# Alternating the first x tiles and the wq/wk slices over two DMA queues, with staggered query steps and gate_w turned on TensorE

## The chip, the cores and the metric

The kernel runs on one core of one Trainium2 chip. The metric is the device time of a run in microseconds (us); lower is better. In the first job the runs of one kernel agree within some tenths of a per cent; in others before alone spread over 1%, and jobs (on different chips of the same kind) can differ too, so times are compared only within one job. TensorE is called PE, VectorE DVE, ScalarE ACT, GpSimd POOL and SyncE SP, as the profile has them.

## The reference, cut to what matters

```python
# x: [1, 2048, 640], wqkv: [640, 1920], gate_w: [640], all bf16
g = sigmoid((x * gate_w).sum(-1))
q, k, v = split(x @ wqkv)            # 32 heads of 20
pq, pk = phi(q), phi(k)              # phi(t) = (t+1 if t>0 else exp(t)) + 1e-6
a = ((pq @ (pk^T v)) / (pq @ sum(pk))) @ wo
b = x1 + gelu(layernorm(x1) @ w3) @ w4,  x1 = x + shifted_gelu_mlp(x)
out = g * a + (1 - g) * b
```

The change touches only how `x @ wq` and `x @ wk` start, and how the column `gate_w` gets beside `wk`, so that the key matmul also gives `x @ gate_w`.

## The kernel before

x is worked on in 16 tiles of 128 tokens. A tile is turned (transposed in five blocks of 128) on PE, evacuated to `xT` by DVE, and then multiplied with five slices of `wq`, 128 rows each; one product of one tile with one slice is a "step" (t, k) of two matmuls, 512 and 128 columns wide, 0.27 us at full rate. The first four tiles are handled slice by slice as the loads land (`q_four`); later tiles come through DMA transposes.

```python
    sch.dma("act", junk[...], A_wqkv[...], "touch")        # 2.5 KB read, result unused
    dma_in(x_tok[:, 0, :], x2[0:128, :], "x0")             # dma_in: on SyncE's queue
    dma_in(x_tok[:, 1, :], x2[128:256, :], "x1")
    load_wq(0)
    dma_in(x_tok[:, 2:4, :], x2[256:512, :]..., "x23")     # x tiles 2 and 3 in one load
    for k in range(1, KD): load_wq(k)
    for k in range(KD): dma_in(wkg[:, k, 0:D], A_wqkv[128 * k:..., D:2 * D], "wk%d" % k)
    dma_in(wkg[:, :, D + 2:D + 3], gate_w..., "gw", noncontig=True)      # 640 pieces of 2 bytes
    # ... cut: the other x tiles, 4 at a time, and their DMA transposes

    WARM = 3200                       # columns of warm-up matmuls on a tile of ones
    def t_x(t):                       # turn x tile t on PE, evacuate it by one DVE copy
        b = bank()
        tr_group(b, [x_tok[:, t, 128 * k:128 * (k + 1)] for k in range(KD)])
        copy(dve, xT[:, :, 128 * t:128 * (t + 1)], psb(b, 0, D)...)

    def q_four():   # (t, k): step of tile t with slice k; (t, None): t_x(t); (None, None): filler matmuls
        order = [(0, 0), (None, None), (1, 0), (2, None), (3, None), (0, 1), (1, 1), (2, 0), (0, 2), (1, 2), (3, 0),
                 (0, 3), (1, 3), (0, 4), (2, 1), (1, 4), (2, 2), (2, 3), (2, 4), (3, 1), (3, 2), (3, 3), (3, 4)]
    # ... cut: warm-up, t_x(0), t_x(1), filler, q_four(), then the key steps of tile 0, and the rest of the kernel
```

## Time and profile before

| what | value | view |
|---|---|---|
| median of 3 runs | 262.18 us (261.81 to 262.46) | times |
| span of the profiled run | 260.0 us | page |
| PE busy | 254.7 us, 98% | page, part 1 |
| PE in the chain that ended last | 97% | page, part 4 |
| first key step begins | 11.26 us | timeline |

From the page: the span, and busy time, share and instruction count of each engine.

```profile
span 260.0 us, 4263 instructions
## 1 busy us (share of the span) xinstructions
PE 254.7 (98%) x1671; PEld 135.9 (52%) x1703; DVE 148.9 (57%) x266; ACT 106.9 (41%) x215; POOL 96.8 (37%) x151
```

The head in the timeline of PE before: start, duration in us, engine, line, what is written from what, number of instructions; in brackets the idle time before and what ended it. L830 are the warm-up and filler matmuls, L611 the turning of x tiles, L857/L858 the two matmuls of a step.

```profile
1.05 2.85 PE L830 MATMUL ps<-xn 128*128 128x512 bf16 x7 [1.05 <-POOL xn L659]
3.69 1.21 PE L611 MATMUL ps<-ident,x_tok 128*128 128x128 bf16 x10
4.73 0.27 PE L830 MATMUL ps<-xn 128*128 128x128 bf16 x2
5.11 0.38 PE L857 MATMUL ps<-wq,xT 128*128 128x512 bf16 x1
...
5.77 0.72 PE L611 MATMUL ps<-ident,x_tok 128*128 128x128 bf16 x10
6.32 0.38 PE L857 MATMUL ps<-wq,xT 128*128 128x512 bf16 x1
...
11.26 0.38 PE L857 MATMUL ps<-wkg,xT 128*128 128x512 bf16 x1
```

Durations overlap, since matmuls are pipelined; the distance from one start to the next is what a thing costs. Ten turned blocks take 1.04 us from 3.69, and 0.55 us from 5.77: PE goes over to twice the rate in between. From 6.32 on, steps follow each other every 0.27 us. After this head the waits view of PE lists only 0.5 us of waiting up to the end, so only what happens before the first key step, and at the tail, can move the end.

The loads of the first 8 us in the DMA view of before: what, queue, count, KB of one, median us from issue to landing.

```profile
wq<-in_A_wqkv_dram SPq DMA_DIRECT2D x5, 160.0 KB, 3.8
...
x_tok<-in_A_x_dram SPq DMA_DIRECT2D x2, 160.0 KB, 2.5
x_tok<-in_A_x_dram SPq DMA_DIRECT2D x1, 320.0 KB, 3.5
```

Taken one by one (issue plus time to landing, good to about 0.1 us), x0 lands at 3.4 us, x1 at 3.6, wq0 at 4.8, x2 and x3 together at 5.7, wq1 at 6.1, wq4 at 7.9.

### The profile page before, as it was taken

To read this page: it belongs to the slowest core of one execution; us is meant where nothing else is said; L and a number is where in the kernel's file an instruction comes from. 1 tells how busy PE (TensorE), PEld (TensorE's weight loads), DVE (VectorE), ACT (ScalarE), POOL (GpSimd) and SP (SyncE) were. 2 spreads that over 40 slices of the span, in tenths; PEclk is the share of its full clock that TensorE was granted. 3 is DMA by queue.
4 is the path that set the end of the run, shared out by engine and by line. 5 is a ranking of instruction groups with operands and counts; after the bars stand their busy time and mean duration, and the time that the engine had idled before them with its cause. 6 is when DMAs were issued, how large, how long until landed. Compare 5 with 4: busy or idle time off the path is not lost.

```text
span 260.0 us, 4263 instructions
## 1 busy us (share of the span) xinstructions
PE 254.7 (98%) x1671; PEld 135.9 (52%) x1703; DVE 148.9 (57%) x266; ACT 106.9 (41%) x215; POOL 96.8 (37%) x151
## 2 busy tenths in 40 slices
PE   8999999999999999999999999999999999999996
PEld 4555555555555454555444545554455544455553
DVE  1597877899903799979994407992033410143333
ACT  1496777741355757674874240005500045100000
POOL 5013995859874017865854202230011100021001
PEclk9999999999999999999999999999999999999999
DMA  6855989642566894355565700232000020000311
GB/s 199 255 103 143 211 149 158 194 87 23 105 126 103 275 377 94 76 101 58 107 124 109 125 0 0 45 85 74 3 0 0 3 101 0 3 0 0 103 50 50
DMA packets 50691, 24.82 MB, mean 95 GB/s; under 512 B 42052, under 2 KB 49261, under 8 KB 50672
## 3 DMA queue, kind: packets, MB, share of 16 engines
q1 hardware_dynamic: 49280, 21.15, 35.8%
q0 software_dynamic: 1152, 3.28, 5.2%
q8 instruction: 13, 0.21, 0.3%
q10 hardware_dynamic: 240, 0.13, 0.2%
q14 instruction: 6, 0.05, 0.1%
HBM read 12.05 MB, written 2.62 MB: 56 GB/s over the span
## 4 chain that ended last, share of the span: by engine, by line
PE 97%; issue 1%; DVE 1%; POOL 0%; POOLq 0%
PE ps L600 61%; PE ps L1106 21%; PE ps L781 8%; PE ps L857 2%; PE ps L830 1%; PE ps L1020 1%; PE ps L1088 1%; DVE x_tok L639 1%; PE ps L858 1%; PE ps L611 1%; PE ps L934 1%; PE ps L1085 0%; POOL xn L659 0%; POOLq L1249 0%
## 5 line engine op out<-in xcount | busy, mean ns | idle before, releaser
L600 PE MATMUL ps<-xnT,w 128*128 128x512 bf16 x349 | 80.7, 379 | 0.5
L1106 PE MATMUL ps<-w,h2T 128*128 128x128 bf16 (+1 forms) x409 | 57.9, 298 | 0.7 <-issue 0.5
L656 ACT ACTIVATE h2T<-ps 128x512 bf16<-128x512 f32 x52 | 30.5, 600 | 65.6 <-PE ps L600 65.5
L600 PEld LDWEIGHTS ps<-xnT,w 128*128 128x128 bf16 x360 | 33.9, 98 | 36.9 <-issue 0.4
L639 DVE SCALAR_TENSOR_TENSOR x_tok<-ps,stg,abx 128x512 bf16<-128x512 f32 (+1 forms) x32 | 17.2, 551 | 61.6 <-PE ps L1106 61.6
L622 POOL TENSOR_SCALAR abx<-x_tok,stg 128x640 f32<-128x640 bf16 x16 | 14.8, 923 | 100.6 <-DVE x_tok L639 95.1
L1106 PEld LDWEIGHTS ps<-w,h2T 128*128 128x128 bf16 x416 | 32.4, 98 | 25.6 <-issue 1.1
L622 POOL TENSOR_SCALAR xn<-x_tok,st 128x640 bf16<-128x640 bf16 x32 | 36.8, 1155 | 15.4 <-DMA xnT<-xn 14.9
L656 ACT ACTIVATE Er<-ps 128x640 bf16<-128x640 f32 x32 | 22.4, 704 | 17.4 <-PE ps L600 8.5
L655 ACT ACTIVATE junk<-x_tok 128x640 bf16<-128x640 bf16 x32 | 23.6, 737 | 4.9 <-DVE x_tok L637 4.4
L656 ACT ACTIVATE hsT<-ps 128x512 bf16<-128x512 f32 (+1 forms) x32 | 18.9, 593 | 15.1 <-PE ps L600 12.7
L600 PE MATMUL ps<-w,hsT 128*128 128x512 bf16 (+1 forms) x159 | 23.8, 298 | 0.1
L600 PE MATMUL ps<-M_sb,pqnT 128*128 128x128 bf16 (+1 forms) x156 | 23.5, 297 | 0.3
L781 PE MATMUL ps<-pk_tok,x_tok 128*128 128x128 bf16 (+1 forms) x156 | 23.3, 297 | 0.2
L639 DVE SCALAR_TENSOR_TENSOR abx<-ps,stg,abx 128x640 f32<-128x640 f32 x16 | 14.1, 884 | 15.3 <-PE ps L600 15.3
L600 PE MATMUL ps<-wkg,xT 128*128 128x512 bf16 (+1 forms) x147 | 22.3, 298 | 0.2
L600 PEld LDWEIGHTS ps<-w,hsT 128*128 128x128 bf16 x160 | 13.3, 98 | 12.3
L600 PEld LDWEIGHTS ps<-M_sb,pqnT 128*128 128x128 bf16 x160 | 13.1, 98 | 10.4
L600 PE MATMUL ps<-wq,xT 128*128 128x512 bf16 (+1 forms) x119 | 18.2, 298 | 0.1
L622 DVE TENSOR_SCALAR Er<-Er 128x640 bf16<-128x640 bf16 x32 | 12.0, 376 | 9.1 <-ACT Er L656 8.8
L637 DVE SCALAR_TENSOR_TENSOR x_tok<-ps,x_tok 128x640 bf16<-128x640 f32 x16 | 13.1, 821 | 6.9 <-PE ps L600 6.0
L600 PEld LDWEIGHTS ps<-wkg,xT 128*128 128x128 bf16 x150 | 12.2, 97 | 9.0
(71 smaller groups left out, 230.0 us busy)
## 6 DMA issues: line engine op xcount, KB each, us to landing
w<-in_B_w_dram SPq DMA_DIRECT2D x1, 2160.0 KB, 8.2
w<-in_B_w_dram SPq DMA_DIRECT2D x1, 2080.0 KB, 13.7
x_tok<-in_A_x_dram SPq DMA_DIRECT2D x3, 640.0 KB, 5.7
out_dram<-x_tok SPq DMA_DIRECT2D x3, 640.0 KB, 3.5
w<-in_B_w_dram POOLq DMA_DIRECT2D x8, 160.0 KB, 4.8
wq<-in_A_wqkv_dram SPq DMA_DIRECT2D x5, 160.0 KB, 3.8
wkg<-in_A_wqkv_dram SPq DMA_DIRECT2D x5, 160.0 KB, 3.9
wv<-in_A_wqkv_dram POOLq DMA_DIRECT2D x1, 800.0 KB, 6.2
```

The source lines that it names most:

```text
L600: ins = e.matmul(out_ap, l, r, start=(i == 0), stop=(i == n - 1))
L611: ins = e.transpose(o, s_, ident[:])
L622: return engf(lambda e: e.tensor_scalar(out_ap, in_ap, s1, s2, op0, op1), rd, [out_ap], cost=cost)
L637: return dve(lambda e: e.scalar_tensor_tensor(out_ap, in0, scalar, in1, op0, op1, accum_out=accum), rd, [out_ap, accum], cost=cost + 70.0)
L639: return dve(lambda e: e.scalar_tensor_tensor(out_ap, in0, scalar, in1, op0, op1), rd, [out_ap], cost=cost)
L655: return act(lambda e: e.activation(out_ap, in_ap, func, bias=bias, scale=scale, accum_out=accum), rd, wr, cost=cost)
L656: return act(lambda e: e.activation(out_ap, in_ap, func, bias=bias, scale=scale), rd, wr, cost=cost)
L781: ins = e.matmul(o, l, r, start=(t0 + q_ == 0), stop=(t0 + q_ == NT - 1))
L830: ins = e.matmul(ps[:, b, 0:n], xn[:, 0, 0:128], xn[:, 0, 0:128].unsqueeze(1).to_broadcast([128, n // 128, 128]), start=True, stop=True)
L857: e.matmul(ps[:, b, 0:512], l, w[:, k, 0:512], start=(k == 0), stop=(k == KD - 1))
L858: return e.matmul(ps[:, b + 1, 0:n2], l, w[:, k, 512:512 + n2], start=(k == 0), stop=(k == KD - 1))
L1106: ins = e.matmul(o, l, r, start=False, stop=(i == KFF - 1), skip_group_check=(n0 > 0))
```

## The change

Intent: fill both issuing queues and let tiles and slices land in the order in which PE wants them, so that PE has steps to do earlier; save the strided gate_w load and the touching read; start the warm-up at once.

```diff
-    sch.dma("act", junk[...], A_wqkv[...], "touch")
-    dma_in(x_tok[:, 0, :], ..., "x0");  dma_in(x_tok[:, 1, :], ..., "x1");  load_wq(0)
-    dma_in(x_tok[:, 2:4, :], ..., "x23")
-    for k in range(1, KD): load_wq(k)
-    for k in range(KD): dma_in(wkg[:, k, 0:D], ..., "wk%d" % k)
-    dma_in(wkg[:, :, D + 2:D + 3], gate_w..., "gw", noncontig=True)
+    sch.dma("pool", gwr[0:KD, :], gate_w.rearrange("(k p) -> k p", p=128), "gw")
+    for t in range(4):
+        load_x(t)                                   # SyncE
+        load_w(wq, "wq", t, 0, "act")               # ScalarE
+    load_w(wq, "wq", 4, 0, "sp")
+    for k in range(KD):
+        load_w(wkg, "wk", k, D, "sp" if k % 2 else "act")
+    for t in range(4, 8): load_x(t)                 # single tiles, then their transposes
...
-    WARM = 3200
+    WARM = 2944
     def t_x(t):
-        # five blocks, one DVE copy
+        for ks in ((0,), (1, 2, 3, 4)) if t < 2 else (range(KD),):
+            # turn the blocks ks into a bank; for t == 3 also gwr as a 5-column matmul into the same bank
+            copy(dve, xT[:, ks[0]:ks[-1] + 1, ...], ...)
+            # for t == 3: copy(dve, wkg[:, :, D + 2:D + 3], ...)
...
     # warm-up and filler: operands are now a ready constant tile of ones, not a tile that POOL writes first
-    order = [(0, 0), (None, None), (1, 0), (2, None), (3, None), (0, 1), (1, 1), (2, 0), (0, 2), ...]
+    order = [(0, 0), (0, 1), (1, 0), (1, 1), (2, None), (0, 2), (2, 0), (1, 2), (2, 1), (3, None), (0, 3), (1, 3), (3, 0), ...]
-    # t_x(0), t_x(1), filler
+    # t_x(0), filler, t_x(1)
```

A comparison of the two programs' instruction order shows that PE does the same things in the same order after these steps.

More of the change, by code (lines that the diff above doesn't have):

```diff
@@ L464, in psb @@
         return ps[:, b, :].bitcast(BF16)[:, n0:n1]
-    ones_c = pa.alloc("ones_c", [128, 768], BF16)
+    ones_c = pa.alloc("ones_c", [128, 128], BF16)
     ident = pa.alloc("ident", [128, 128], BF16)
@@ L470, in _build @@
     negh = pa.alloc("negh", [128, 4], F32)
+    gwr = pa.alloc("gwr", [8, 128], BF16)
     st1 = pa.alloc("st1", [128, 8, NT], F32)
@@ L674, in dma_in, with load_x, load_w, x_transpose @@
         return sch.dma("sp", out_ap, in_ap, key, **kw)
-    sch.dma("act", junk[0:16, 0, 0:80].rearrange("p (k f) -> p k f", k=KD),
-            A_wqkv[:, 0:16].rearrange("(k e r) f -> e r k f", k=KD, r=8)[:, 0, :, :], "touch")
-    dma_in(x_tok[:, 0, :], x2[0:128, :], "x0")
-    dma_in(x_tok[:, 1, :], x2[128:256, :], "x1")
-    def load_wq(k):
-        dma_in(wq[:, k, :], A_wqkv[128 * k:128 * (k + 1), 0:D], "wq%d" % k)
-    load_wq(0)
-    dma_in(x_tok[:, 2:4, :], x2[256:512, :].rearrange("(n p) d -> p n d", p=128), "x23")
-    for k in range(1, KD):
-        load_wq(k)
-    for k in range(KD):
-        dma_in(wkg[:, k, 0:D], A_wqkv[128 * k:128 * (k + 1), D:2 * D], "wk%d" % k)
-    dma_in(wkg[:, :, D + 2:D + 3], gate_w.rearrange("(k p o) -> p k o", p=128, o=1), "gw", noncontig=True)
-    for c in range(1, NCH):
+    def load_x(t):
+        dma_in(x_tok[:, t, :], x2[128 * t:128 * (t + 1), :], "x%d" % t)
+    def load_w(dst, name, k, c0, queue):
+        sch.dma(queue, dst[:, k, 0:D], A_wqkv[128 * k:128 * (k + 1), c0:c0 + D], "%s%d" % (name, k))
+    def x_transpose(t):
+        sch.dma("sp", xT[:, :, 128 * t:128 * (t + 1)], x_tok[:, t, :], "trx%d" % (t % 4), transpose=True)
+    sch.dma("pool", gwr[0:KD, :], gate_w.rearrange("(k p) -> k p", p=128), "gw")
[3 more added lines that the diff above has]
+    load_w(wq, "wq", 4, 0, "sp")
+    for k in range(KD):
+        load_w(wkg, "wk", k, D, "sp" if k % 2 else "act")
+    for t in range(4, 8):
+        load_x(t)
+    for t in range(4, 8):
+        x_transpose(t)
+    for c in range(2, NCH):
         dma_in(x_tok[:, 4 * c:4 * c + 4, :], x2[512 * c:512 * (c + 1), :].rearrange("(n p) d -> p n d", p=128), "xc%d" % c)
         for t in range(4 * c, 4 * c + 4):
-            sch.dma("sp", xT[:, :, 128 * t:128 * (t + 1)], x_tok[:, t, :], "trx%d" % (t % 4), transpose=True)
+            x_transpose(t)
     k_done = {}
@@ L716, in load_wvo @@
             sch.dma("pool", wo_aug[0:n, r, :], A_wo[R6 * r:R6 * r + n, :], "wo", group_total=6, deps=dp)
-    memset(pool, xn[:, 0, 0:128], 1.0)
     memset(pool, ones_c[:], 1.0)
@@ L740, in _build @@
     IT = _Items()
-    WARM = 3200
+    WARM = 2944
     WARM2 = 256
     def t_x(t):
-        b = bank()
-        tr_group(b, [x_tok[:, t, 128 * k:128 * (k + 1)] for k in range(KD)])
-        src = psb(b, 0, D).rearrange("p (k c) -> p k c", k=KD)
-        dst = xT[:, :, 128 * t:128 * (t + 1)]
-        copy(dve, dst, src)
+        for ks in ((0,), (1, 2, 3, 4)) if t < 2 else (range(KD),):
+            b = bank()
+            tr_group(b, [x_tok[:, t, 128 * k:128 * (k + 1)] for k in ks])
+            if t == 3:
+                pe(lambda e: e.matmul(ps[:, b, 448:448 + KD], gwr[0:KD, :], ident[0:KD, 0:KD], start=True, stop=True),
+                   [gwr[0:KD, :], ident[:]], [ps[:, b, 448:448 + KD]], cost=60.0)
+            copy(dve, xT[:, ks[0]:ks[-1] + 1, 128 * t:128 * (t + 1)],
+                 psb(b, 0, 128 * len(ks)).rearrange("p (k c) -> p k c", k=len(ks)))
+            if t == 3:
+                copy(dve, wkg[:, :, D + 2:D + 3], ps[:, b, 448:448 + KD].rearrange("p (k o) -> p k o", o=1))
     def phi(b, dst, after_exp=None):
@@ L829, in fn @@
             for n in steps:
-                ins = e.matmul(ps[:, b, 0:n], xn[:, 0, 0:128], xn[:, 0, 0:128].unsqueeze(1).to_broadcast([128, n // 128, 128]), start=True, stop=True)
+                ins = e.matmul(ps[:, b, 0:n], nc.const_aps.tensor(1.0, [128, 128], BF16), nc.const_aps.tensor(1.0, [128, n], BF16),
+                               start=True, stop=True)
             return ins
-        pe(fn, [xn[:, 0, 0:128]], [ps[:, b, :]], cost=cols * cyc)
+        pe(fn, [], [ps[:, b, :]], cost=cols * cyc)
     def q_tile(t):
@@ L864, in q_four @@
     def q_four():
-        order = [(0, 0), (None, None), (1, 0), (2, None), (3, None), (0, 1), (1, 1), (2, 0), (0, 2), (1, 2), (3, 0), (0, 3), (1, 3), (0, 4),
-                 (2, 1), (1, 4), (2, 2), (2, 3), (2, 4), (3, 1), (3, 2), (3, 3), (3, 4)]
+        order = [(0, 0), (0, 1), (1, 0), (1, 1), (2, None), (0, 2), (2, 0), (1, 2), (2, 1), (3, None), (0, 3), (1, 3), (3, 0), (0, 4),
+                 (2, 2), (1, 4), (2, 3), (2, 4), (3, 1), (3, 2), (3, 3), (3, 4)]
         stream(order, wq, 128, lambda t, b: phi(b, pq_tok[:, t + 1, :]))
@@ L879, in _build @@
     addA(("warm",), 0.0, lambda: warmup(WARM, 0.834))
-    for i in range(2):
-        addA(("tx", i), 0.28, lambda i=i: t_x(i))
+    addA(("tx", 0), 0.28, lambda: t_x(0))
     addA(("warm", 1), 0.0, lambda: warmup(WARM2, 0.42))
+    addA(("tx", 1), 0.28, lambda: t_x(1))
     addA(("q", 3), 5.44, q_four)
```

## The prediction

> **What bounds the kernel.** TensorE. The page's busy table has PE at 254.7 us of a 260.0 us span (98%), the clock row shows full grant, and PE has 97% of the chain that ended last. The waits view gives PE 1.1 us for POOL at the start and 0.5 us of issue. Only time saved at head or tail moves the end. The change touches the head; a comparison of instruction order shows PE's order unchanged after the query steps of the first four tiles.
>
> **The head today (timeline).** PE fills with warm-up matmuls from 1.05 to 3.7 us while x tiles 0 and 1 land (issued 0.79 and 1.23 us, 2.4 to 2.6 us to landing). Ten transposes run from 3.69 to 4.73, about 104 ns each; the next ten, from 5.77, take 0.56 us, so PE was at half rate in the first group. The Trainium skill ("TensorE: Matmul & The Clock Gate", What's actually happening) has the array at half clock until about 3.4 us of sustained work; the trace agrees, the change falling between 3.69 and 5.1 us. Then come two fillers, a gap before 5.11, a step, a filler, a step; PE is dense only from 5.77. The first key step starts at 11.23 after 0.19 us idle: it also waits for gate_w, issued at 6.97 with 4.2 us to landing, so about 11.17.
>
> **Removed, added, moved.** Useful PE work from the first transpose to the first key step: 20 transposes and 20 steps of 0.27 us, about 7.0 us; today it takes 7.5. Removable: 0.5 us of fillers, gaps and gate wait, plus 0.2 to 0.3 us because the warm-up reads a ready constant and begins near 0.8 us, so full clock comes earlier too. Against it: one filler stays (0.1 to 0.2 us), a 5-column matmul (under 0.05 us), three small DVE copies.
> Loads: SyncE issued 11 small loads, 0.43 us each, up to 6.97 us. With two queues the last wq slice is issued near 2.6 instead of 4.1 us. But transfers share one bandwidth (345 GB/s from 4 to 8 us, DMA view; 0.47 us per 164 KB slice), and the Trainium skill ("DMA: Bandwidth & Descriptors", Issuing engines are not separate DMA queues) says a second issuer saves only issue time. So x0 lands at 3.3 to 3.5 us as now, x1 later (near 4.1, sharing with wq0), wq4 near 7.0: just ahead of the staggered steps.
> gate_w through GpSimd costs about 0.9 us of POOL (eight w1 loads took 7.20), so the identity is ready near 2.3 us, not 2.0: harmless. ScalarE issues seven loads to about 4 us; its first exp is due near 8.5. Tiles 4 to 7 are transposed earlier than 13.16 us; PE did not wait for them.
>
> **On the critical path:** the first key step at about 10.6 us instead of 11.23, everything behind it 0.6 us earlier.
>
> **Prediction:** 261.6 us, 261.0 to 262.3 in 8 of 10 cases. Faster by over 2%: 0.01; within 2%: 0.98; slower by over 2%: 0.01.
>
> **What will show it.** Warm-up from about 0.8 us; first transposes at 3.3 to 3.5; first query step near 4.7; first key step at 10.3 to 10.9 without a gate_w wait; last PE instruction earlier by as much. DMA view: first loads issued before 5 us, rate still near 345 GB/s.
>
> **What would make it wrong.** x1 or wq1 landing after 4.5 us, through sharing with wq0, or because the small touching read of wqkv was of use (3.05 to 4 us has only about 140 GB/s); a gap that lowers the PE clock; the identity later than 3.4 us; DVE evacuation holding the staggered steps.

## The result, and the profile after

The changed kernel took 262.81 us (median of 6 runs, 262.46 to 263.89), before took 262.25 us (6 runs, 261.81 to 262.7). The ratio is 1.0026 with a 95% interval of 1.0006 to 1.0047: slower by a quarter of a per cent, where 0.2% faster had been forecast. (Ratios here are the mean time of one kernel's fast runs over that of the other's of the same rounds, so not quite the ratio of the quoted medians.)

The page after:

```profile
span 261.1 us, 4300 instructions
## 1 busy us (share of the span) xinstructions
PE 257.3 (99%) x1703; PEld 135.7 (52%) x1703; DVE 149.2 (57%) x269; ACT 106.8 (41%) x215; POOL 96.0 (37%) x151
```

PE's busy time rose by 2.6 us, but that is no finding: 32 more PE records are in this trace, and some matmul records can be missing from a trace. The timeline of PE after tells more (L841 is warm-up and filler, L612 the turning of x tiles, L869/L870 a step, L755 the gate_w matmul):

```profile
0.83 2.61 PE L841 MATMUL ps<-const-bfloat16-1.0 128*128 128x512 bf16 x8 [0.83 <-PEq L1261]
3.81 0.71 PE L612 MATMUL ps<-ident,x_tok 128*128 128x128 bf16 x5 [0.36 <-DMA x_tok<-in_A_x_dram]
...
4.53 0.69 PE L612 MATMUL ps<-ident,x_tok 128*128 128x128 bf16 x5
5.06 0.38 PE L869 MATMUL ps<-wq,xT 128*128 128x512 bf16 x1
...
6.40 0.45 PE L612 MATMUL ps<-ident,x_tok 128*128 128x128 bf16 x5
6.69 0.38 PE L869 MATMUL ps<-wq,xT 128*128 128x512 bf16 x1
...
7.44 0.39 PE L869 MATMUL ps<-wq,xT 128*128 128x512 bf16 x1 [0.32 <-DVE xT L666]
...
8.27 0.44 PE L612 MATMUL ps<-ident,x_tok 128*128 128x128 bf16 x5
8.64 0.17 PE L755 MATMUL ps<-ident,gwr 5*128 5x5 bf16 x1
8.75 0.39 PE L869 MATMUL ps<-wq,xT 128*128 128x512 bf16 x1
...
9.49 0.39 PE L869 MATMUL ps<-wq,xT 128*128 128x512 bf16 x1
...
12.31 0.38 PE L869 MATMUL ps<-wkg,xT 128*128 128x512 bf16 x1
```

The first key step begins at 12.31 us instead of 11.26, 1.05 us later. The last group of PE begins at 255.32 instead of 254.26 us, 1.06 us later. So the whole loss of this profile arose before the first key step, and nothing was won or lost behind it. The last group, before and then after:

```profile
254.26 3.69 PE L1106 MATMUL ps<-w,h2T 128*128 128x512 bf16 x26
```

```profile
255.32 3.69 PE L1118 MATMUL ps<-w,h2T 128*128 128x512 bf16 x26
```

One caution: a profile is one draw. The profiled run of before took 261.42 us, less than any of its six runs in the first job; e10 below, with the same loads and steps, has its first key step at 12.00 us. So 1.05 us is what separates these two profiles, not the loss of a typical run (0.56 us between the medians).

Where it arose can be read from starts. The first query step begins at 5.06 us (5.11 before): equal. From there to the first key step, 20 steps and two groups of turned blocks need 20 x 0.27 + 2 x 0.29 = 6.0 us at full rate. Before took 6.15 us for it, after 7.25. The excess of 1.2 us after is made up of these gaps, each a start less the preceding start and cost:

| gap | us | what ended it |
|---|---|---|
| before x tile 2 is turned (6.14 to 6.40) | 0.26 | x2 lands at 6.3 to 6.4 |
| before step (2,0) (6.96 to 7.44) | 0.48 | the DVE copy of x tile 2, begun at 6.89, 0.49 us long |
| from the end of x tile 3's turning to step (0,3) (8.55 to 8.75) | 0.20 | the gate_w matmul |
| before step (3,0) (9.30 to 9.49) | 0.19 | the DVE cast of gate_w, right behind the DVE copy of x tile 3 |
| before the first key step (12.22 to 12.31) | 0.09 | issue |

The DVE copies of x tiles 2 and 3, the cast, and the weight load of PE that opens step (3,0):

```profile
6.89 0.49 DVE L666 COPY xT<-ps 128x640 bf16<-128x640 bf16 x1 [1.21 <-PE ps L612]
8.85 0.49 DVE L666 COPY xT<-ps 128x640 bf16<-128x640 bf16 x1 [1.47 <-PE ps L755]
9.26 0.17 DVE L666 CAST wkg<-ps 128x5 bf16<-128x5 f32 x1
9.49 0.10 PEld L869 LDWEIGHTS ps<-wq,xT 128*128 128x128 bf16 x1 [0.36 <-DVE wkg L666]
```

Queues in the DMA view, 6 to 8 us, before and then after (packets, MB, share of the time of the 16 engines):

```profile
DMA packets 599, 0.68 MB, mean 340 GB/s; under 512 B 68, under 2 KB 599, under 8 KB 599
...
q1 hardware_dynamic: 599, 0.68, 103.7%
```

```profile
DMA packets 627, 0.71 MB, mean 355 GB/s; under 512 B 73, under 2 KB 627, under 8 KB 627
...
q1 hardware_dynamic: 312, 0.35, 51.6%
q10 hardware_dynamic: 315, 0.36, 50.8%
```

One queue already had the engines busy all the time; two queues share the same bandwidth in equal halves. That agrees with the Trainium skill ("DMA: Bandwidth & Descriptors", Queues, rings and completion order), by which each DMA engine goes round-robin over the queues that have work, packet by packet, and the rate is close to the limit of about 358 GB/s that the same page gives for one core's memory reads (Specifications): 355 is measured here, though 362 in e8 below, so the figure is no hard bound. So x0 shares with wq0 and lands at 3.8 us instead of 3.4, x1 at 4.5 instead of 3.6, x2 at 6.3 and x3 at 7.3 instead of 5.7; wq1 lands at 4.7 instead of 6.1, and wq4 at 8.1 instead of 7.9.

### The profile page after: what moved, and what is told of

Same layout as the page of the kernel before. It is cut to its first block, busy times and chain, and to the rows that moved or that the text cites. A ratio compares the mean times of both kernels' runs of the same rounds, so it can differ in the third digit from the quotient of the medians.

```text
span 261.1 us, 4300 instructions
## 1 busy us (share of the span) xinstructions
PE 257.3 (99%) x1703; PEld 135.7 (52%) x1703; DVE 149.2 (57%) x269; ACT 106.8 (41%) x215; POOL 96.0 (37%) x151
## 4 chain that ended last, share of the span: by engine, by line
PE 96%; DMA 2%; DVE 1%; SPq 0%; issue 0%
PE ps L601 61%; PE ps L1118 21%; PE ps L792 8%; PE ps L869 2%; DMA x_tok<-in_A_x_dram 2%; PE ps L1032 1%; PE ps L1100 1%; DVE x_tok L640 1%; PE ps L946 1%; PE ps L870 0%; SPq L285 0%; PE ps L612 0%; DVE xT L666 0%; PE ps L1097 0%; PE ps L755 0%
## 5 line engine op out<-in xcount | busy, mean ns | idle before, releaser
L601 PE MATMUL ps<-xnT,w 128*128 128x512 bf16 x360 | 82.3, 379 | 0.0
L1118 PE MATMUL ps<-w,h2T 128*128 128x512 bf16 (+1 forms) x416 | 58.8, 299 | 0.0
L623 POOL TENSOR_SCALAR xn<-x_tok,st 128x640 bf16<-128x640 bf16 x32 | 35.6, 1120 | 15.4 <-DMA xnT<-xn 14.9
L601 PE MATMUL ps<-M_sb,pqnT 128*128 128x512 bf16 (+1 forms) x160 | 24.3, 299 | 0.0
L792 PE MATMUL ps<-pk_tok,x_tok 128*128 128x512 bf16 (+1 forms) x160 | 23.9, 299 | 0.0
L792 PEld LDWEIGHTS ps<-pk_tok,x_tok 128*128 128x128 bf16 x160 | 12.4, 98 | 8.4
```

Of the source, the lines that this page charges most:

```text
L601: ins = e.matmul(out_ap, l, r, start=(i == 0), stop=(i == n - 1))
L623: return engf(lambda e: e.tensor_scalar(out_ap, in_ap, s1, s2, op0, op1), rd, [out_ap], cost=cost)
L792: ins = e.matmul(o, l, r, start=(t0 + q_ == 0), stop=(t0 + q_ == NT - 1))
L1118: ins = e.matmul(o, l, r, start=False, stop=(i == KFF - 1), skip_group_check=(n0 > 0))
```

## The experiments

Eighteen runs, of fourteen new kernels and of the changed one again, were made in five jobs (e3b repeats e3, e4b repeats e4, e16 repeats e13). All results were correct against the reference. "Key" is the start of the first key step in the profiled run, "full" the time from which PE's matmuls are seen at full rate (a 512-column matmul listed at 0.38 us and followed after 0.22, not at 0.63 and after 0.43).

| job | kernel | median us (range; runs) | ratio to before (95%) | key | full |
|---|---|---|---|---|---|
| 1 | before | 262.25 (261.81-262.7; 6) | | 11.26 | 4.7 |
| 1 | changed | 262.81 (262.46-263.89; 6) | 1.0026 (1.0006-1.0047) | 12.31 | 5.0 |
| 2 | before | 262.96 (261.7-267.17; 7) | | | |
| 2 | e1_oldorder | 264.96 (263.4-265.84; 4) | 1.0062 (0.9984-1.014) | 13.15 | 4.5 |
| 2 | e2_onequeue | 263.98 (262.96-264.61; 4) | 1.0027 (0.996-1.0095) | 14.36 | 9.9 |
| 2 | e3_split | 262.3 (261.94-263.3; 4) | 0.9979 (0.9899-1.0058) | 11.69 | 4.3 |
| 2 | e4_oldloads | 262.95 (262.03-453.89; 4) | 0.998 (0.9901-1.006) | (clock 0.56) | |
| 3 | before | 262.34 (262.06-266.19; 11) | | | |
| 3 | e4b_oldloads | 262.28 (262.06-263.05; 6) | 0.9977 (0.9937-1.0017) | 12.02 | by 5.3 |
| 3 | e5_gwold | 262.49 (262.11-263.86; 4) | 0.9989 (0.9926-1.0053) | 12.87 | 7.1 |
| 3 | e6_bridge | 262.82 (262.66-263.05; 4) | 0.9995 (0.9946-1.0044) | 12.43 | 5.3 |
| 3 | e7_notouch | 262.28 (262.02-262.6; 6) | 0.9975 (0.9935-1.0014) | 12.17 | by 5.4 |
| 4 | before | 263.08 (262.25-266.22; 11) | | | |
| 4 | e8_again | 264.0 (263.06-264.92; 6) | 1.0039 (1.0011-1.0066) | 13.94 | 8.5 |
| 4 | e3b_split | 264.01 (262.31-264.38; 6) | 1.0036 (1.0008-1.0064) | 11.95 | 5.9 |
| 4 | e9_split_gwold | 263.1 (262.38-263.99; 6) | 1.0005 (0.9979-1.0031) | 12.65 | 7.4 |
| 4 | e10_warmup | 263.28 (261.77-263.7; 6) | 1.0005 (0.9976-1.0035) | 12.0 | by 5.4 |
| 5 | before | 264.08 (261.96-266.0; 11) | | | |
| 5 | e11_longwarm | 263.28 (262.38-263.73; 6) | 0.9993 (0.9953-1.0034) | 12.34 | 4.3 |
| 5 | e12_longwarm_split | 262.76 (262.31-263.63; 6) | 0.9979 (0.994-1.0019) | 12.03 | 4.8 |
| 5 | e13_longwarm_split_gwold | 262.2 (261.49-262.93; 6) | 0.9965 (0.9922-1.0007) | 11.15 | by 4.2 |
| 5 | e14_before_shortwarm | 262.44 (262.24-265.3; 6) | 0.9989 (0.994-1.0039) | 11.97 | 6.9 |
| 6 | before | 262.21 (261.82-266.8; 11) | | | |
| 6 | e15_shortwarm | 263.78 (263.63-264.32; 6) | 1.0056 (1.0026-1.0086) | 13.46 | 8.5 |
| 6 | e16_best_again | 262.66 (261.97-263.42; 6) | 1.0007 (0.9976-1.0038) | 11.88 | 4.8 |

(Job 1 is the measurement of the change itself; 2 to 6 are the five jobs of experiments.) Medians and ranges are of all runs; each of jobs 2 to 6 has one slow run of before (266.0 to 267.17 us, granted clock 0.994), and e4 one at 453.89 us, which the ratios leave out. Before spread more in jobs 2 to 6 than in the first, so that most intervals hold 1. So most of the argument is read from the heads of the profiles, one execution each; where two variants of one job can be told apart by their times, that is said.

### The order of steps: e1_oldorder

```diff
-        order = [(0, 0), (0, 1), (1, 0), (1, 1), (2, None), (0, 2), (2, 0), ...]
+        order = [(0, 0), (None, None), (1, 0), (2, None), (3, None), (0, 1), ...]     # as before; loads as changed
```

> The changed kernel with one part undone: the query steps of the first four tiles in the order of before (tiles 2 and 3 transposed together after two steps); loads, warm-up and gate_w as in the changed kernel. Theory A, the landings rule: x tile 3 lands near 7.3 us in the changed kernel's trace (issued 2.2, 5.1 us to landing) and wq1 no sooner than 4.8, so with tiles 2 and 3 transposed before the third step PE stands still from about 5.7 to 7.3 us, and the first key step comes at 12.6 to 13.0 us, later than the 12.31 of the changed kernel. Theory B, the new order of steps is what costs: first key step at 11.6 us or earlier.

Its timeline of PE at the turning of x tiles 2 and 3:

```profile
6.18 0.45 PE L612 MATMUL ps<-ident,x_tok 128*128 128x128 bf16 x5 [0.31 <-DMA x_tok<-in_A_x_dram]
7.56 0.45 PE L612 MATMUL ps<-ident,x_tok 128*128 128x128 bf16 x5 [0.93 <-DMA x_tok<-in_A_x_dram]
```

The first key step came at 13.15 us, a little past A's 12.6 to 13.0. Theory A's mechanism holds: with the new loads the old order waits 1.1 us for x3. The staggered order is needed by the alternating loads; it is not the culprit by itself.

### One queue or two: e2_onequeue and e6_bridge

```diff
-        load_w(wq, "wq", t, 0, "act")
+        load_w(wq, "wq", t, 0, "sp")
-        load_w(wkg, "wk", k, D, "sp" if k % 2 else "act")
+        load_w(wkg, "wk", k, D, "sp")
```

> The changed kernel with all loads on the SyncE queue, in the same alternating order x0, wq0, x1, wq1 and so on. Theory A1, two queues halve each other's rate and so delay the x tiles: with one queue x0 lands at 3.4 us instead of 3.8, x2 and x3 at least 0.5 us earlier than 6.3 and 7.3, and the first key step is at 11.7 us or earlier. Theory A2, it is the alternating order itself that puts x2 fifth and x3 seventh: x2 lands at 5.8 to 6.3 and x3 at 7.0 to 7.5 as well with one queue, and the first key step stays at 12.0 to 12.4 us.

On one queue x0 landed at 3.0 us and wq0 at 3.7, but x1 only at 5.0, x2 at 6.0, x3 at 7.1 and wq4 at 8.4. So sharing costs x0 0.7 to 0.8 us (in all profiles x0 lands by 3.4 us with one queue and not before 3.7 with two). For x2 and x3 no cost can be told: they came up to 0.4 us earlier here, but at 6.3 and 7.8 us in e6 below, with the same loads. That x2 comes near 6 and x3 past 7 us is the doing of the alternating order (A2), in which x2 is the fifth slice and x3 the seventh. But the first key step came at 14.36 us, which neither theory had. The timeline of PE shows why:

```profile
3.77 0.42 PE L841 MATMUL ps<-const-bfloat16-1.0 128*128 128x128 bf16 x2
5.02 0.72 PE L612 MATMUL ps<-ident,x_tok 128*128 128x128 bf16 x5 [0.83 <-DMA x_tok<-in_A_x_dram]
5.53 0.63 PE L869 MATMUL ps<-wq,xT 128*128 128x512 bf16 x1
```

PE stood idle for 0.83 us before x1, and then the steps ran at half rate (0.54 us each, 512-column matmuls listed at 0.63) until 9.9 us. This gave a new theory, H: the idle time kept the PE clock down. e6 fills that gap with filler and changes nothing else:

```diff
-    WARM2 = 256
+    WARM2 = 1536      # on top of e2_onequeue
```

> The kernel of e2_onequeue with the filler between x tiles 0 and 1 made longer (1536 columns instead of 256, about 1.3 us at half rate), so that PE does not stand idle from 4.19 to 5.02 us. Theory H, that idle time kept the PE clock at half rate until 9.9 us in e2_onequeue (512-column matmuls 0.43 us apart): with the bridge PE is at full rate by 7 us at the latest, and the first key step comes at 11.9 to 12.6 us instead of 14.36. Theory I, the clock comes up at a time of its own whatever PE does: half rate until after 8 us in this run too.

```profile
5.45 0.38 PE L869 MATMUL ps<-wq,xT 128*128 128x512 bf16 x1
```

Full rate came at 5.3 us and the first key step at 12.43: H holds here, I does not. With the clock up, one queue gives nearly the key step of two (12.31), near the 12.0 to 12.4 of theory A2.

### The evacuation of x tiles 2 and 3: e3_split and e3b_split

```diff
-        for ks in ((0,), (1, 2, 3, 4)) if t < 2 else (range(KD),):
+        for ks in ((0,), (1, 2, 3, 4)) if t < 4 else (range(KD),):
```

> The changed kernel with the evacuation of x tiles 2 and 3 split as that of tiles 0 and 1 (first 128 columns by themselves, 0.23 us instead of 0.49). Theory B1, the wait for the DVE copy after a lone transpose (0.48 us before step (2,0), about 0.2 before step (3,0)) is a real part of the loss: first key step 0.3 to 0.6 us earlier, at 11.7 to 12.0. Theory A, only landings rule: the time saved is waited for at the next landing (x tile 3), first key step no more than 0.15 us earlier.

```profile
6.31 0.45 PE L612 MATMUL ps<-ident,x_tok 128*128 128x128 bf16 x5 [0.15 <-DMA x_tok<-in_A_x_dram]
6.62 0.39 PE L869 MATMUL ps<-wq,xT 128*128 128x512 bf16 x1
...
6.90 0.38 PE L869 MATMUL ps<-wq,xT 128*128 128x512 bf16 x1
```

Step (2,0) follows 0.28 us after step (0,2) (6.62 to 6.90), where the changed kernel had 0.75 us (6.69 to 7.44). The stretch from the first query step (4.91) to the first key step (11.69) is 6.78 us instead of 7.25: 0.47 us won, about the wait that was taken away. B1 holds in the profile.

> The kernel of e3_split (evacuation of x tiles 2 and 3 in two pieces as well) once more with five rounds, beside the changed kernel. Theory B1: 0.3 to 0.8 us below the changed kernel's median of the same job, and no wait for DVE before step (2,0). Theory A: the same time as the changed kernel within 0.2 us.

In the second job the wait was again gone (key at 11.95 us), but the median equalled that of the changed kernel (264.01 and 264.0). As for the time, B1 missed. The runs ranged from 262.31, which was the profiled one, to 264.38; the runs without a profile can't be looked into. That PE was at half rate in many of them would hide the gain, but this is only argued.

### What is left when loads and order are undone: e4_oldloads, e4b_oldloads, e7_notouch, e10_warmup

e4 and e4b are the same kernel: the changed kernel with loads, touching read and order of before; gate_w on PE, split copies and warm-up stay.

> The changed kernel with two parts undone: loads of before (one queue, x2 and x3 as one load in fourth place, with the small touching read) and the order of steps of before. What stays of the change: gate_w turned on PE, warm-up from the constant and shorter, tiles 0 and 1 evacuated in two pieces. Theory A: these parts are good or neutral, and the first key step is at 10.9 to 11.2 us, before the 11.26 of before (no gate_w wait, 0.19 us). Theory C, gate_w on PE and the split copies cost more than they give: first key step at 11.3 us or later.

The profile fell in a run of 453.89 us at a granted clock of 0.56, so it was run again.

> The kernel of e4_oldloads once more, since its profile fell in a run at a granted clock of 0.56 (452.6 us), from which nothing can be read. Same theories: A, first key step at 10.9 to 11.2 us and a time of 0.1 to 0.4 us below before; C, 11.3 us or later.

The first key step came at 12.02 us, so A missed and C was met in the profile, but not for one reason only: in this run wq0 landed at 5.2 us (4.8 in before) and x2/x3 at 6.1 (5.7). From the turning of tiles 2 and 3 to the next step it took 0.77 us (6.14 to 6.91) instead of 0.55, with the gate_w matmul in between, and step (2,0) then waited another 0.2 us. The time was that of before (ratio 0.9977, interval holding 1).

> The kernel of e4_oldloads without the small touching read of wqkv on the ScalarE queue. Theory T, that read was of use: without it wq0 lands later than 4.9 us (it landed at 4.9 in e4_oldloads) and the first query step is later. Theory U, it is itself the cause of the poor rate from 3.0 to 4.0 us (113 to 143 GB/s in before and e4_oldloads, which have it; 249 to 384 in the changed kernel and e2_onequeue, which have not): without it wq0 lands by 4.4 us, the load of x tiles 2 and 3 by 5.4 instead of 5.8, and the first key step is 0.2 to 0.5 us earlier than in e4b_oldloads.

Without the touching read wq0 landed at 5.4 us instead of 5.2, x2/x3 at 6.3 instead of 6.1, key at 12.17; the time did not move. U is refuted (from 3.5 to 4 us the rate was 146 GB/s without it too), and T's 0.2 us is no more than what landings differ by from run to run. Why the rate is poor from 3 to 4 us in kernels with the loads of before is open.

e10 is before with the warm-up of the change alone (constant operand, start at 0.83 us, 2944 columns).

> Before, with the warm-up part of the change alone: it reads the ready constant, starts near 0.83 instead of 1.05 us and is 256 columns shorter. Theory W: the earlier start brings the full PE clock earlier and is worth 0.1 to 0.3 us. Theory V: when the clock comes up does not follow the start of the warm-up by a fixed time (5.0 us in both before and the changed kernel, though the second started 0.2 us earlier), so the median is that of before within 0.15 us.

W's gain does not show: 263.28 against 263.08 us, just outside V's 0.15 us, with an interval (0.9976 to 1.0035) too wide to exclude 0.1 to 0.3 us. In the profile the clock did not come up earlier: two filler matmuls at 4.37 us were still at half rate (0.41 us; 0.27 at 4.73 in before). And the first query step waited for wq0 until 5.35 us, so that an earlier clock had nothing to give here. This run has the loads and steps of before, yet wq0 landed at 5.3 us (4.8 in before), x2 and x3 at 6.3 (5.7), gate_w at 11.9 (11.2), and the first key step came at 12.00: so far can such differences in landing move it.

### gate_w on PE: e5_gwold

```diff
-    sch.dma("pool", gwr[0:KD, :], ...)                          # and its matmul and copy in t_x(3)
+    dma_in(wkg[:, :, D + 2:D + 3], gate_w..., "gw", noncontig=True)     # behind the wk slices, as before
```

> The changed kernel with gate_w loaded as in before (strided, straight into the weight tile, on SyncE behind the wk slices) and so without the small matmul and its evacuation beside x tile 3. Theory C, gate_w on PE costs in the head: the 0.10 us matmul and the wait for its cast (step (3,0) waited 0.2 us) fall away, first key step 0.2 to 0.4 us earlier than the 12.31 of the changed kernel. Theory D, it is hidden: first key step within 0.1 us of 12.31.

From the turning of x tile 3 to step (0,3) it took 0.28 us (9.02 to 9.30) instead of 0.48 in the changed kernel (8.27 to 8.75): the gate_w matmul costs PE 0.20 us. The wait before step (3,0) stayed at 0.20 us, here put down to the copy of x tile 3. In the changed kernel the copy begins 0.10 us after step (0,3), here 0.20, and the cast ends last (9.43). An estimate: step (2,0) began 0.06 us after its copy ended, so the copy alone would have let step (3,0) begin at 9.40, and about half of its wait is the cast. In all, without gate_w on PE step (3,0) follows the turning 0.20 us sooner (1.02 us instead of 1.22). The expected earlier key step did not come, because PE was at half rate until 7.1 us in this run (key at 12.87).

### The changed kernel again: e8_again

> The changed kernel itself once more, beside the variants below, for a second profile of its head. Theory E (the waits come from the order of loads and steps, so they return): x2 lands near 6.3 us and step (2,0) again waits 0.4 to 0.5 us for the evacuation of x tile 2; the time is 0.1 to 0.4% above before. Theory F (chance of one profile): no such wait.

```profile
4.21 0.71 PE L612 MATMUL ps<-ident,x_tok 128*128 128x128 bf16 x5 [0.77 <-DMA x_tok<-in_A_x_dram]
...
5.61 0.63 PE L869 MATMUL ps<-wq,xT 128*128 128x512 bf16 x1
...
9.07 0.39 PE L869 MATMUL ps<-wq,xT 128*128 128x512 bf16 x1 [0.18 <-DVE xT L666]
```

Time (0.39% above before) and the wait for DVE return, though the wait is shorter. The new thing is that x0 landed at 4.2 us, PE stood 0.77 us, and ran at half rate until about 8.5 us; key at 13.94 us. The windows view of the same run (start and end, length, then busy time of PE, PEld, DVE, ACT, POOL, granted clock, DMA share, GB/s) shows nothing of it:

```profile
5.61:8.28 2.67, 2.67 (x16) 1.55 (x14) 0.47 (x2) 0.00 (x0) 0.00 (x0) 1.00 1.03 362
```

PE counts as fully busy and the granted clock reads 1.00 while every matmul takes twice as long. This half rate is seen in the durations alone.

### The gap before x0: e11_longwarm, e15_shortwarm, e14_before_shortwarm

Changed kernel with one number changed, both ways, and before with a shorter warm-up:

```diff
-    WARM = 2944
+    WARM = 4096      # e11_longwarm;  1024 in e15_shortwarm
-    WARM = 3200
+    WARM = 2048      # e14_before_shortwarm, in the kernel of before
```

> The changed kernel with one number changed: warm-up of 4096 columns instead of 2944, so that at half rate it lasts from 0.83 to about 4.24 us and PE has no gap while x0 lands (3.8 to 4.2 us). Theory H: that gap (0.36 us in the changed kernel's first profile, 0.77 in e8_again, 0.65 in e9_split_gwold) is what keeps PE at half rate until 7 or 8 us in many of its runs; with the long warm-up the first query step runs at full rate (512-column matmul listed at 0.38, not 0.63 us), before 5.6 us, the median falls by 0.5 us or more below e8_again's excess over before (so to within 0.3 us of before), and the runs spread less. Theory I, the clock comes up at a time of its own: half-rate steps as often as without, and the same excess of about 0.4% over before.

```profile
0.83 3.57 PE L841 MATMUL ps<-const-bfloat16-1.0 128*128 128x512 bf16 x8 [0.83 <-PEq L1261]
...
5.10 0.38 PE L869 MATMUL ps<-wq,xT 128*128 128x512 bf16 x1
```

> The changed kernel with a warm-up of 1024 columns instead of 2944: at half rate it ends near 1.7 us, and PE stands idle for about 2 us until x tile 0 lands. The opposite of e11_longwarm. Theory H (idle time before x0 delays the full PE clock): query steps at half rate until 7 us or later (512-column matmul listed at 0.63 us), first key step at 13.2 us or later, and a median at least 0.6% above before. Theory I (the clock comes up at a time of its own, or the warm-up is too short to matter): full rate by 5.5 us as in e11_longwarm, time as of the changed kernel.

```profile
3.88 0.71 PE L612 MATMUL ps<-ident,x_tok 128*128 128x128 bf16 x5 [2.04 <-DMA x_tok<-in_A_x_dram]
...
5.13 0.63 PE L869 MATMUL ps<-wq,xT 128*128 128x512 bf16 x1
```

With the gap filled, the first query step runs at full rate, and the changed kernel stands at 0.9993 of before; with a gap of 2.04 us the steps run at half rate until 8.5 us, the key step comes at 13.46, and the time is 0.56% above before, with all six runs between 263.63 and 264.32 us. H holds in both profiles. In time e15 is clear of before (the expected 0.6% was missed by little) but not of the changed kernel, whose intervals (1.0006 to 1.0047, and 1.0011 to 1.0066 in e8) overlap that of e15 (1.0026 to 1.0086). The interval of e11 (0.9953 to 1.0034) holds 1 and overlaps those of the changed kernel too, because before spread from 261.96 to 266.0 in that job. So what the gap costs in time is not shown.

> The kernel of before with a warm-up of 2048 columns instead of 3200, which at half rate ends near 2.75 us and leaves a gap of about 0.6 us before x0 lands at 3.4: the gap of the changed kernel put into the kernel of before, whose loads and steps are otherwise untouched. Theory H: the median rises by 0.4 us or more over before, and the profile shows half-rate query steps in at least some runs (512-column matmuls at 0.63 us after 5.1 us). Theory I: same time as before within 0.2 us.

Its profile has the half rate as H says (512-column matmul at 5.67 us listed at 0.63; full at 6.9), but the time did not rise: 262.44 against 264.08 us for before. H's expectation for the time missed. Before's runs in this job came in two groups, near 262 and near 264 to 265 us, and what made the second group is not known; so in the kernel of before the price of the gap is not shown.

### Repairs together: e9, e12, e13, e16

e9 is split copies and gate_w as before; e12 long warm-up and split copies; e13 and e16 are one kernel with all three.

> e3_split with gate_w loaked as in before (no small matmul, no cast beside x tile 3): the candidate for the best version. If gate_w on PE costs 0.1 us of matmul and 0.2 us of waiting for the cast as the traces say: first key step 0.2 to 0.35 us before that of e3b_split at the same clock (11.69 in e3_split), and a median below both before and the changed kernel by 0.3 us or more. If it is hidden: equal to e3b_split.

> Both repairs: long warm-up and the evacuation of x tiles 2 and 3 in two pieces. If the two losses are of separate kinds they add: first key step at 11.5 to 11.9 us, and a median 0.3 to 0.6 us below e11_longwarm, about that of before or up to 0.3 us below it. If one hides the other: within 0.15 us of e11_longwarm.

> As e12_longwarm_split, and gate_w loaded as in before: the best that the runs so far point to. First key step at 11.2 to 11.6 us, median 0.2 to 0.6 us below before. If gate_w beside x tile 3 costs nothing here, it equals e12_longwarm_split within 0.15 us.

> The kernel of e13_longwarm_split_gwold a second time, since before's own runs spread over 4 us in that job. If it is truly better than before: ratio below 1 again, a median 0.2 to 0.6 us below before's, first key step at 11.1 to 11.6 us. If e13's result was chance: ratio within 0.1% of 1.

e9 had a gap of 0.65 us before x0 and half rate until 7.4 us, key at 12.65: no gain over before (1.0005), though its median is 0.9 us below those of e8 and e3b in the same job. In the next job the medians of e11, e12 and e13 fell in the expected steps: 263.28, 262.76, 262.2 us. The single steps are not clear of noise. What is clear, twice, is the pair of split copies and old gate_w together: the mean of e9 is 0.89 us below that of e8 (standard error 0.33), and that of e13 0.91 below that of e11 (0.31), six runs each. The table of gaps gives 0.48 + 0.20 + 0.19 = 0.87 us for just these parts; with split copies alone the means fall by 0.34 and 0.37 us (errors 0.41 and 0.30), which is not clear. e13 had the earliest first key step of all (11.15 us), and was at 0.9965 of before, interval just holding 1. On another chip the same kernel was at 1.0007 of before, x3 landing at 8.0 us instead of 6.6, key at 11.88. So split copies and the old gate_w take back what the change lost, but a version better than before is not shown.

### The gap and the clock over all profiles

| PE idle before x0 or x1 lands | profiles | PE at full rate from (us) |
|---|---|---|
| none listed | before, e4b, e6, e7, e10, e11, e12, e13, e16 | 4.2 to 5.4 |
| 0.35 to 0.54 us | changed, e1, e3, e3b, e5, e14 | 5.0, 4.5, 4.3, 5.9, 7.1, 6.9 |
| 0.65 to 0.83 us | e9, e8, e2 | 7.4, 8.5, 9.9 |
| 2.04 us | e15 | 8.5 |

The Trainium skill ("TensorE: Matmul & The Clock Gate", What's actually happening) has the array go to full clock after a busy window of about 3.4 us, and the window running free of the kernel's start. The trace agrees: without a gap the change comes 3.3 to 4.6 us after the first matmul; with a gap it may come as early, or up to a window or more later, and no fixed time after the start. In the six latest (e2, e5, e8, e9, e14, e15) it comes 3.3 to 4.9 us after PE resumed work. The table counts only gaps before x0 or x1: e4b, e7 and e10 stood still later, 0.48 to 0.70 us until wq0 landed, after 3.9 us or so of unbroken work, and ran at full rate right behind that gap.

## Why the prediction was right or wrong

- Right: PE bounds the kernel, only the head moves, and what the head loses or wins appears unchanged at the end (1.05 us at the first key step, 1.06 at the last group). Right too: within 2%; the bandwidth near 345 GB/s and shared; the warm-up from 0.83 us; no harm from the GpSimd issue (identity ready at 2.6 us); no gate_w wait (though by the starts of PE that wait was only 0.05 us in before's profile, 11.21 to 11.26, and not 0.19; it was 0.22 in e10).
- Wrong, the step that failed: "So x0 lands at 3.3 to 3.5 us as now, x1 later (near 4.1, sharing with wq0), wq4 near 7.0: just ahead of the staggered steps." x0 landed at 3.8 (4.2 in the second profile), x1 at 4.5, wq4 at 8.1, and the landing of x2 and x3, which PE needs for half of its steps, was not worked out at all: 6.3 and 7.3 us. x2 cost a wait of 0.26 us. e2 and e6 show that this is mostly the alternating order; sharing adds 0.7 to 0.8 us to x0. e1 shows that loads and order of steps can't be judged apart.
- Wrong, a cost left out: the prediction had "three small DVE copies" as a cost off the path. The copies of x tiles 2 and 3, which did not change, went onto the path, because the new order leaves one step (tile 2) or two (tile 3) between a tile's turning and its first use: 0.48 us before (2,0), and 0.19 before (3,0), there together with the cast of gate_w. ("DVE evacuation holding the staggered steps" was named as a danger, but given no cost.) e3 took the first away and won 0.47 us in the profile; its repeat e3b showed no gain in time. Before had hidden the same 0.49 us copy behind another tile's turning and two steps.
- Wrong, a size: "a 5-column matmul (under 0.05 us)" cost 0.20 us (e5: 0.28 instead of 0.48 us). Together these two points are 0.87 us of the table, and undoing both won 0.89 and 0.91 us in time (e9 against e8, e13 against e11).
- Wrong: "so full clock comes earlier too", and 0.2 to 0.3 us for it. e10 shows nothing won, within its noise. The warm-up was shortened to end near 3.4 us while x0 was made later, which opens a gap; in e8 the full rate came at 8.5 us, while in the changed kernel's first profile the gap of 0.36 us did no harm (5.0 us). That gaps do this is shown by e6, e11 and e15 in the profiles, one each; what it costs in time is not shown. The danger had been named ("a gap that lowers the PE clock") but given no weight.
- The sum: predicted key step 10.6 us. Measured 12.31: the first query step at 5.06 instead of 4.7 (0.36), and 7.25 us from there instead of 5.9 (1.35), of which the gaps of the table are 1.22.
- Open: what makes before's own runs fall into two groups in some jobs; why landings of the same load differ by up to 1.5 us from run to run (x3 in e13 and e16); how often PE is at half rate in runs without a profile.

## What to carry to other kernels

A second DMA queue gave next to no bandwidth where the first had the engines busy (355 against 340 GB/s); it reordered landings, so write down when each tile lands and let every step wait for its own tile before believing in a new order. When steps are staggered to follow the loads, look at what each of them had hidden: a copy that takes 0.49 us was free behind another tile's turning and two steps, and on the path behind one step. Let the warm-up of TensorE last until the first operand has surely landed, since 0.83 us of idle time went with a first key step 1.9 us later (14.36 in e2, 12.43 in e6), and read half rate from matmul durations, not from the granted clock.

## What the Trainium skill lacked or had wrong

- "TensorE: Matmul & The Clock Gate" (HAM oscillation) warns of idle gaps over about 3.4 us. The page asks for a sustained busy window before the first release of the clock, but not how short a gap spoils it: after 0.77 and 0.83 us of idle time PE was at half rate until 8.5 and 9.9 us (e8, e2), without the gap until 5.3 (e6); 0.36 and 0.54 us did no harm in two profiles (e3, e1), 0.35 did in one (7.1 us, e5).
- No page says that the granted clock of such a profile can read 1.00 while matmuls run at half rate (e8, 5.61 to 8.28 us: 0.63 us listed for a 512-column matmul, 0.38 later).
- "DMA: Bandwidth & Descriptors" (Issuing engines are not separate DMA queues) says rightly that a second issuer adds no engines, but not what it takes from the first: x0 landed 2.2 to 2.6 us after its issue with one queue (e2, before), 3.0 to 3.4 us with a second queue issuing beside it (changed kernel, e8).
